# Moving a row copy from GpSimd to ScalarE, and a second buffer for a half of the hidden layer

## The chip, the cores and the metric

The kernel runs on one core of a Trainium2 chip. The metric is device time in microseconds (us): the median of several runs. The engines are called here as the profile calls them: PE (TensorE), DVE (VectorE), ACT (ScalarE), POOL (GpSimd) and SP, which issues loads. DMAs are issued from the queues of SP, ACT and POOL.

## The reference

Block-causal attention over 8 batches, 8 heads, 576 tokens and a head width of 64 gives 4608 rows of 512 values. A mixture of experts follows, with one expert out of 8 for each row:

```python
logits = x @ w_gate
expert_idx = np.argmax(logits, axis=1)
gate_w = probs[np.arange(N), expert_idx]
for e in range(E):
    mask = expert_idx == e
    h = np.maximum(x[mask] @ w1[e], 0.0)       # 512 -> 1024
    out[mask] = gate_w[mask, None] * (h @ w2[e])   # 1024 -> 512
```

All is fp32. The kernel keeps that accuracy by splitting each operand of the expert layers into a high part (a type that PE multiplies in one pass) and a low part (the rest), and adds three products: high by high, low by high, high by low.

## The kernel before

The first 366 us or so are attention, with the routing of each batch woven in; rows go to a table in DRAM (`xd`), sorted slots of 128 rows of one expert follow. The change lies in the second part, class `Experts`. It runs 38 slots in the profiled execution; slot `t` takes part in several **periods**, and `period(t)` (L1160) writes down the order of all engines by hand. Each engine's queue runs in that order, and counting semaphores tie the queues together.

In one period **PE** does 48 products of 512 columns and 4 transposes: `first_pe(t)` (L963, first layer of slot t, two halves of 12 into the banks `ph` and `o`), `second_pe(t-1, 0)` (L1086, 12 products of the second layer of the slot before), `hidden_pe(t, 1)` (L1059, turns the second half of the hidden values), and `second_pe(t-1, 1)`.

**The rows of a slot** come by `gather` (L874, an indirect DMA on POOL into one of four buffers `xg`), three periods ahead. From the sixth slot on (`TURNED` = 5) they are turned by DMA: POOL splits the 32-bit words into two 16-bit planes `xq` (`rows_planes`, L936), ACT issues the transposing DMA into `xt` (`rows_turned`, L945), POOL joins the planes again into `xf` (`rows_joined`, L951), ACT takes the high part (`rows_high`, L958) and POOL the low part (`rows_pool`, L925).

**The hidden values** (1024 per row) are two halves. The first half goes by DMA too: ACT's `planes` (L1023) reads `ph` and writes the planes into `h[0]`, `turned` (L1035) issues the transpose into `hf`, `joined` (L1046) writes the words back into `h[0]`, `joined_high` (L1053) takes the high part and the relu in place, and POOL subtracts the low part (`hidden_low`, L1080). The second half goes by `relu_act` (L1015) into `h[1]`, by `hidden_pe`, and by `hidden_act` (L1068), which reads the turned values from PSUM; POOL subtracts its low part first. Since `h[0]` is one buffer, `planes(t)` waits until POOL has finished the last low part of slot t-1 (`hp` at 2t).

The order of a period, from L1160 on:

- ACT: `out_act(t-2)` (L1114, scales the result by the gate), `planes(t)`, `turned(t)`, `relu_act(t, 1)`, `rows_high(t+1)`, `rows_turned(t+2)`, `hidden_act(t, 1)`, `joined(t)`, `joined_high(t)`.
- POOL: `out_pool(t-2)` (L1126, drain and the store by indirect DMA), `gather(t+3)`, `rows_joined(t+1)`, `gate(t+2)` and the planes of `rows_planes(t+2)`, `rows_pool(t+1)`, then the low parts of the second and of the first half.
- DVE splits each expert's weights (60 chunks, a cast for the high part at L1239, a subtraction for the low part at L1245), paced by PE's progress; SP loads them. POOL takes no part in that.

The last period is followed by `finish` (L1200): both halves of the last second layer, the last two stores.

Of the kernel before, what the change touches and what calls it, by code (L numbers as in the profile page):

```python
# [794 lines left out]
class Experts:  # L795
# [9 lines left out]
    def __init__(self, ctx, tc, ident, w1, w2, out, router, high, low, y, raw, ph):  # L805
        self.tc, self.nc, self.router = tc, tc.nc, router
        self.w1, self.w2, self.out, self.xd = w1, w2, out, router.xd
        self.ident, self.stab, self.nslot = ident, router.stab, router.nslot
        self.xg, meta = router.xg, router.meta
        self.e8, self.off, self.col, self.row, self.before = (*(meta[k] for k in ("e8", "off", "col", "row")), meta["si"])  # L810
        self.high, self.low = high, low
        self.hh, self.hl = low[:2], low[2:]
        sb = ctx.enter_context(tc.tile_pool(name="moe", bufs=1))
        ps = ctx.enter_context(tc.tile_pool(name="moeps", bufs=1, space=PSUM))

        def t(name, shape, dt=F32):
            return sb.tile(shape, dt, tag=name, name=name)

        self.w = t("w", [P, 2, 4, 4096], F32R)
        self.raw = raw  # L820
        self.idx = t("idx", [P, router.nslot + 2], I32)
        self.xf, self.xq, self.xt = t("xf", [P, 512]), t("xq", [P, 1024], U16), t("xt", [P, 1024], U16)
        self.gates = t("gates", [P, 8])
        self.h, self.hf = [t("h0", [P, 512]), t("h1", [P, 512])], t("hf", [P, 512])
        self.y = y

        def b(name):
            return ps.tile([P, 512], F32, tag=name, name=name)
# [28 lines left out]
    def run(self):  # L857
# [8 lines left out]
            )  # L866
        }
        sraw = [tc.alloc_semaphore(f"raw{i}") for i in range(nr)]
        sg = [tc.alloc_semaphore(f"g{i}") for i in range(4)]
        sy = tc.alloc_semaphore("y")  # L870
        pe, act, dve, pool, sp = nc.tensor, nc.scalar, nc.vector, nc.gpsimd, nc.sync
        wf = self.w.rearrange("p a b c -> p (a b c)")

        def gather(t):  # L874
            i = t % 4
            if t < EARLY or t >= NS:
                return
            if t == EARLY:
# [4 lines left out]
            c = pool.value_load(self.col[t : t + 1, 0:1], min_val=0, max_val=TC - 1)  # L883
            pool.tensor_copy(self.idx[:, t : t + 1], self.stab[:, bass.ds(c, 1)]).then_inc(sem["v1"], 1)  # L884
            pool.wait_ge(sem["v1"], t + 1 - EARLY)
            if t >= 4:
                pool.wait_ge(sem["gc"], t - 3)
                if t - 4 < TURNED:
                    pool.wait_ge(sem["xt"], t - 4)
                else:  # L890
                    pool.wait_ge(sem["xq"], t - 3 - TURNED)
            pool.indirect_dma_start(  # L892
                out=self.xg[i],
                out_offset=None,
# [3 lines left out]

        def gathered(t):

            return len([k for k in range(EARLY, t + 1) if k % 4 == t % 4])

        def rows_in(t):

            if t >= EARLY:
                pe.wait_ge(sg[t % 4], 16 * gathered(t))
            if t >= 2:
                pe.wait_ge(sem["xa"], 2 * t - 2)
            for k in range(4):
                m = pe.transpose(self.px[:, P * k : P * k + P], self.xg[t % 4][:, P * k : P * k + P], self.ident)  # L910
# [19 lines left out]

        def gate(t):
            if t >= EARLY:
                pool.wait_ge(sg[t % 4], 16 * gathered(t))
            pool.tensor_copy(self.gates[:, t % 8 : t % 8 + 1], self.xg[t % 4][:, GATE : GATE + 1]).then_inc(sem["gc"], 1)

        def rows_planes(t):  # L936
            gate(t)
            if t > TURNED:
                pool.wait_ge(sem["ti"], 16 * (t - TURNED))
            pool.tensor_copy(  # L940
                self.xq.rearrange("p (o c) -> p o c", o=2),
                self.xg[t % 4][:, 0:DM].bitcast(U16).rearrange("p (c o) -> p o c", o=2),
            ).then_inc(sem["xq"], 1)

        def rows_turned(t):  # L945
# [3 lines left out]
            act.dma_start_transpose(self.xt.rearrange("p (k c) -> p k c", c=P), self.xq).then_inc(sem["ti"], 16)  # L949

        def rows_joined(t):  # L951
            pool.wait_ge(sem["ti"], 16 * (t - TURNED + 1))
            pool.wait_ge(sem["xa"], 2 * t - 2)
            pool.tensor_copy(  # L954
                self.xf.bitcast(U16).rearrange("p (c o) -> p o c", o=2), self.xt.rearrange("p (o c) -> p o c", o=2)
            ).then_inc(sem["xj"], 1)

        def rows_high(t):  # L958
# [64 lines left out]
        def planes(t):  # L1023

            act.wait_ge(sem["mm1"], 2 * t + 2)
            if t == 2:
                act.wait_ge(sem["ht"], 3)
            else:
                act.wait_ge(sem["hp"], 2 * t)
            act.copy(  # L1030
                self.h[0].bitcast(U16).rearrange("p (o c) -> p o c", o=2),
                self.ph[0].bitcast(U16).rearrange("p (c o) -> p o c", o=2),
            ).then_inc(sem["ra"], 1)

        def turned(t):  # L1035
# [6 lines left out]
            act.dma_start_transpose(  # L1042
                self.hf.bitcast(U16).rearrange("p (k c) -> p k c", c=P), self.h[0].bitcast(U16)
            ).then_inc(sem["tr"], 16)

        def joined(t):  # L1046
            act.wait_ge(sem["tr"], 16 * (t - 1))
            act.copy(  # L1048
                self.h[0].bitcast(U16).rearrange("p (c o) -> p c o", o=2),
                self.hf.bitcast(U16).rearrange("p (o c) -> p c o", o=2),  # L1050
            ).then_inc(sem["jo"], 1)

        def joined_high(t):  # L1053
            act.wait_ge(sem["jo"], t - 1)
            act.wait_ge(sem["mm2"], t)
            act.activation(self.hh[t % 2][:, 0], self.h[0], AF.Relu).then_inc(sem["ha"], 1)  # L1056
            act.activation(self.h[0], self.h[0], AF.Relu).then_inc(sem["ha"], 1)

        def hidden_pe(t, f):  # L1059
            if t:  # L1060
# [19 lines left out]
        def hidden_low(t, f, engine):  # L1080
            n = f if t < 2 else 1 - f
            engine.wait_ge(sem["ha"], 4 * t + 2 * n + 2)
            hh, hl = self.hh[t % 2][:, f], self.hl[t % 2][:, f]
            engine.tensor_sub(hl, self.hf if t < 2 else self.h[f], hh).then_inc(sem["hp"], 1)  # L1084

        def second_pe(t, part):  # L1086
            e8, off = self.regs[t]
# [72 lines left out]
        def period(t):  # L1160
# [39 lines left out]
        def finish(t):  # L1200
# [10 lines left out]
            for i in range(4):  # L1211
                n = len([k for k in range(EARLY, min(last + 3, NS)) if k % 4 == i])
                if n:
                    pool.wait_ge(sg[i], 16 * n)

# [2 lines left out]
        with tc.tile_critical():  # L1218
# [34 lines left out]
            sp.dma_start(self.router.by_partition(last, GATE, GATE + 1), g[:, 0:4, None]).then_inc(sem["ga"], 16)  # L1253
            sp.dma_start(self.xd[t0 : t0 + 64, GATE : GATE + 1], g[0:64, 4:5]).then_inc(sem["ga"], 16)
            begin()
            for i in range(5):
                if i == 1:
                    rows_pool(1)
                self.router.scatter(last, i, posi).then_inc(sem["sc"], 16)
            rows_pool(2)  # L1260
            for t in range(EARLY):
                gate(t)
            gather(EARLY)
            for k in range(4):
                m = dve.tensor_copy(tuple(self.parts(0, k))[1], self.low[k].rearrange("p a b -> p (a b)"))
# [188 lines left out]
```

## Time and profile before

| what | value |
|---|---|
| median of 3 runs | 878.25 us (875.03 to 879.1) |
| the profiled execution's own time | 875.0 us |
| its span | 873.2 us |
| mean granted clock of PE | 0.981 of full speed |
| PE busy | 816.7 us, 94% |
| ACT busy | 541.9 us, 62% |
| POOL busy | 445.9 us, 51% |
| DVE busy | 437.2 us, 50% |

The span runs from the first to the last instruction, and 1.8 us lie around it. A timeline row has the start in us from the span's start, the length in us, the engine, the line, the operation, the tiles (out <- in) and how often it stands merged in the row; in brackets stands how long the engine was idle before it and what released it. `ACTq` is ACT's queue issuing a DMA. Ends of PE's matmuls are modelled, so PE is better read from start to start. A tile name loses its number: `h` is either buffer of the hidden half.

### The profile page before, as it was taken

To read this page: it belongs to the slowest core of one execution; us is meant where nothing else is said; L and a number is where in the kernel's file an instruction comes from. 1 tells how busy PE (TensorE), PEld (TensorE's weight loads), DVE (VectorE), ACT (ScalarE), POOL (GpSimd) and SP (SyncE) were. 2 spreads that over 40 slices of the span, in tenths; PEclk is the share of its full clock that TensorE was granted. 3 is DMA by queue.
4 is the path that set the end of the run, shared out by engine and by line. 5 is a ranking of instruction groups with operands and counts; after the bars stand their busy time and mean duration, and the time that the engine had idled before them with its cause. 6 is when DMAs were issued, how large, how long until landed. Compare 5 with 4: busy or idle time off the path is not lost.

```text
span 873.2 us, 16347 instructions
## 1 busy us (share of the span) xinstructions
PE 816.7 (94%) x4990; PEld 620.9 (71%) x4990; DVE 437.2 (50%) x1208; ACT 541.9 (62%) x1220; POOL 445.9 (51%) x503
## 2 busy tenths in 40 slices
PE   6999999999999999898999999897898989999995
PEld 5777777777777777686877777665676667777773
DVE  5778787878787877587064000367338523000000
ACT  6898899898988898344445544434353444554452
POOL 3000223333233222447776777676767777677763
PEclk8999999999999999999999999999999989999998
DMA  6254848372636281448558443569658663344342
GB/s 208 94 133 136 167 118 186 108 160 95 161 107 149 95 231 40 107 146 252 131 153 185 97 91 90 158 163 192 170 133 269 177 152 83 68 92 97 85 75 63
DMA packets 120747, 118.24 MB, mean 135 GB/s; under 512 B 82577, under 2 KB 85905, under 8 KB 120658
## 3 DMA queue, kind: packets, MB, share of 16 engines
q1 hardware_dynamic: 38082, 78.26, 31.9%
q10 hardware_dynamic: 74976, 18.62, 14.1%
q0 software_dynamic: 7600, 20.24, 7.2%
q8 instruction: 49, 0.80, 0.4%
q14 instruction: 40, 0.33, 0.1%
HBM read 77.02 MB, written 21.98 MB: 113 GB/s over the span
## 4 chain that ended last, share of the span: by engine, by line
PE 39%; POOL 22%; issue 15%; POOLq 7%; ACT 6%; ACTq 5%; DMA 2%; DVE 1%; DVEq 0%
PE o L305 11%; POOL low L1084 5%; POOLq L1127 5%; ACTq L949 5%; POOL xf L954 5%; PE ya L203 5%; POOL xg L892 4%; POOL xq L940 4%; PE xa L203 3%; PE py L1104 3%; PE o L340 2%; ACT h L1078 2%; DMA kd<-kT 2%; PE o L983 2%; PE ph L983 1%
## 5 line engine op out<-in xcount | busy, mean ns | idle before, releaser
L1104 PE MATMUL py<-w,low 128*128 (+1 forms) x912 | 231.3, 404 | 7.5 <-ACT low L1056 4.7
L1104 PEld LDWEIGHTS py<-w,low 128*128 128x128 f32 x912 | 171.5, 192 | 46.2 <-issue 8.3
L1239 DVE CAST w<-raw 128x1024 fp32r<-128x1024 f32 x60 | 58.3, 1021 | 196.5 <-PE o L983 136.0
L1084 POOL TENSOR_TENSOR low<-h,low 128x512 fp32r<-128x512 f32 x72 | 102.5, 1424 | 82.3 <-ACT h L1078 47.8
L248 POOL TENSOR_SCALAR p<-p,rs 128x64 f32<-128x64 f32 x32 | 14.2, 443 | 250.1 <-DVE rs L244 167.5
L983 PE MATMUL ph<-w,high 128*128 x408 | 107.7, 410 | 12.8 <-POOL high L929 6.5
L983 PEld LDWEIGHTS ph<-w,high 128*128 128x128 f32 x408 | 76.1, 193 | 40.0 <-POOL high L929 14.6
L983 PE MATMUL o<-w,high 128*128 x408 | 101.5, 398 | 0.0
L1245 DVE TENSOR_TENSOR w<-raw,w 128x1024 fp32r<-128x1024 f32 x60 | 91.3, 1579 | 2.2 <-PE o L983 2.2
L983 PEld LDWEIGHTS o<-w,high 128*128 128x128 f32 x408 | 77.8, 191 | 18.6
L961 ACT CAST high<-xf 128x512 fp32r<-128x512 f32 x34 | 21.1, 620 | 77.7 <-POOL xf L954 77.7
L1075 ACT CAST low<-pt 128x512 fp32r<-128x512 f32 x40 | 23.5, 588 | 72.8 <-issue 43.6
L1129 POOL DMA_INDIRECT out<-y,idx x35 | 43.0, 1229 | 44.0 <-issue 39.0
L1030 ACT COPY h<-ph 128x1024 uint16<-128x1024 uint16 x36 | 36.4, 1012 | 37.6 <-POOL low L1084 37.6
L1021 ACT ACTIVATE h<-o 128x512 f32<-128x512 f32 x37 | 22.1, 598 | 55.2 <-issue 45.2
L235 ACT ACTIVATE pb<-ya,neg 128x320 f32<-128x320 f32 (+2 forms) x93 | 48.5, 532 | 2.3 <-PE pt30x L274 1.6
L733 POOL DMA_INDIRECT tab<-toks,posi x40 | 41.6, 1041 | 15.1 <-issue 14.0
L235 ACT ACTIVATE pb<-yb,neg 128x320 f32<-128x320 f32 (+2 forms) x93 | 49.3, 544 | 0.0
L892 POOL DMA_INDIRECT xg<-xd,idx x38 | 43.5, 1145 | 10.5 <-POOL idx L884 10.5
L1048 ACT COPY h<-hf 128x1024 uint16<-128x1024 uint16 x36 | 42.6, 1183 | 7.8 <-DMA hf<-h 7.8
L929 POOL TENSOR_TENSOR high<-xf,high 128x512 fp32r<-128x512 f32 x35 | 45.7, 1305 | 2.7 <-ACT xf L923 2.7
L954 POOL COPY xf<-xt 128x1024 uint16<-128x1024 uint16 x34 | 47.0, 1383 | 0.0
(968 smaller groups left out, 2081.4 us busy)
## 6 DMA issues: line engine op xcount, KB each, us to landing
raw<-w SPq DMA_DIRECT2D x60, 512.0 KB, 5.4
qd<-qT SPq DMA_DIRECT2D x32, 352.0 KB, 2.8
v<-vt SPq DMA_DIRECT2D x32, 352.0 KB, 4.6
kd<-kT SPq DMA_DIRECT2D x32, 288.0 KB, 3.4
xd<-xt SPq DMA_DIRECT2D x7, 1026.0 KB, 11.0
xd<-xg SPq DMA_DIRECT2D x9, 256.5 KB, 7.2
xg<-w SPq DMA_DIRECT2D x8, 256.0 KB, 4.7
xd<-x SPq DMA_DIRECT2D x8, 128.0 KB
```

What stands on the lines that cost most here:

```text
L203: ins = mm(out, q[x][r, 128 * (i - 1) : 128 * i], q[y][r, o : o + w], start=n == 0, stop=n == 2, skip_group_check=True,)
L235: ins = self.nc.scalar.activation(dst, src, AF.Exp, bias=self.neg[m][:, c : c + 1], scale=1.0, accum_out=self.sums[m][:, c : c + 1])
L305: self.nc.tensor.matmul(out[r], self.raws[m][2][:, slot], self.ph[m, bank][:, c0:c1], start=t in (0, 5), stop=t in (4, 5), skip_group_chec ...
L892: pool.indirect_dma_start(out=self.xg[i], out_offset=None, in_=self.xd[:, :], in_offset=bass.IndirectOffsetOnAxis(ap=self.idx[:, t : t + 1 ...
L929: pool.tensor_sub(self.x(t, 1), self.xf, self.x(t, 0)).then_inc(sem["xp"], 1)
L949: act.dma_start_transpose(self.xt.rearrange("p (k c) -> p k c", c=P), self.xq).then_inc(sem["ti"], 16)
L954: pool.tensor_copy(self.xf.bitcast(U16).rearrange("p (c o) -> p o c", o=2), self.xt.rearrange("p (o c) -> p o c", o=2)).then_inc(sem["xj"], 1)
L983: m = pe.matmul(self.ph[f], x[:, P * k : P * k + P], weights(k, f, part), start=start and k == 0, stop=stop and k == 3,)
L1084: engine.tensor_sub(hl, self.hf if t < 2 else self.h[f], hh).then_inc(sem["hp"], 1)
L1104: m = pe.matmul(self.py[t % 2], h[:, c // 4, P * (c % 4) : P * (c % 4) + P], wf[:, bass.ds(off + (base + 512 * c), 512)], start=n == 0, st ...
L1239: dve.tensor_copy(hi, raw[m % nr]).then_inc(sem["wh"], 1)
L1245: dve.tensor_sub(lo, raw[m % nr], hi).then_inc(sem["wd"], 1)
```

## The change

`rows_joined` moves from POOL's queue to ACT's, ahead of `rows_high`, with its access pattern in the word order that `joined` uses. The first half of the hidden values alternates between `h[0]` and the memory of the fourth row buffer `xg[3]`; `planes(t)` waits for the low part of slot t-2 in place of t-1. The gathered rows take three buffers in turn instead of four. The three early gate copies stand ahead of the table's scatters, as the buffer of slot 0 is now the first to be gathered into.

```diff
+        self.hz = [self.h[0], self.xg[3][:, 0:512]]
...
         def gather(t):
-            i = t % 4
+            i = t % 3
...
-            if t >= 4:
-                pool.wait_ge(sem["gc"], t - 3)
-                if t - 4 < TURNED:
-                    pool.wait_ge(sem["xt"], t - 4)
-                else:
-                    pool.wait_ge(sem["xq"], t - 3 - TURNED)
+            pool.wait_ge(sem["gc"], t - 2)
+            if t - 3 < TURNED:
+                if t > 3:
+                    pool.wait_ge(sem["xt"], t - 3)
+            else:
+                pool.wait_ge(sem["xq"], t - 2 - TURNED)
...
         def rows_joined(t):
-            pool.wait_ge(sem["ti"], 16 * (t - TURNED + 1))
-            pool.wait_ge(sem["xa"], 2 * t - 2)
-            pool.tensor_copy(
-                self.xf.bitcast(U16).rearrange("p (c o) -> p o c", o=2), self.xt.rearrange("p (o c) -> p o c", o=2)
+            act.wait_ge(sem["ti"], 16 * (t - TURNED + 1))
+            act.wait_ge(sem["xp"], t - 1)
+            act.copy(
+                self.xf.bitcast(U16).rearrange("p (c o) -> p c o", o=2), self.xt.rearrange("p (o c) -> p c o", o=2)
             ).then_inc(sem["xj"], 1)
...
         def planes(t):
             act.wait_ge(sem["mm1"], 2 * t + 2)
-            if t == 2:
+            if t < 4:
                 act.wait_ge(sem["ht"], 3)
             else:
-                act.wait_ge(sem["hp"], 2 * t)
+                act.wait_ge(sem["hp"], 2 * t - 2)
             act.copy(
-                self.h[0].bitcast(U16).rearrange("p (o c) -> p o c", o=2),
+                self.hz[t % 2].bitcast(U16).rearrange("p (o c) -> p o c", o=2),
...
             elif more:
+                rows_joined(t + 1)
                 rows_high(t + 1)
...
-            if more and t + 1 >= TURNED:
-                rows_joined(t + 1)
...
             begin()
+            for t in range(EARLY):
+                gate(t)
             for i in range(5):
                 if i == 1:
                     rows_pool(1)
                 self.router.scatter(last, i, posi).then_inc(sem["sc"], 16)
             rows_pool(2)
-            for t in range(EARLY):
-                gate(t)
             gather(EARLY)
```

`turned`, `joined`, `joined_high` and `hidden_low` take `hz[t % 2]` in place of `h[0]` in the same way, and every other `% 4` of the row buffers becomes `% 3`.

## Rows read from the trace of the kernel before

**Rows 1.** Parts 1 and 2 of the page: busy us; busy tenths by slice

```profile
PE 816.7 (94%) x4990; PEld 620.9 (71%) x4990; DVE 437.2 (50%) x1208; ACT 541.9 (62%) x1220; POOL 445.9 (51%) x503
...
POOL 3000223333233222447776777676767777677763
```

**Rows 2.** Part 4 of the page: the chain that ended last, shares by engine

```profile
PE 39%; POOL 22%; issue 15%; POOLq 7%; ACT 6%; ACTq 5%; DMA 2%; DVE 1%; DVEq 0%
```

**Rows 3.** Timeline of PE: start, length, instruction, [idle before]; ph begins a period

```profile
411.59 2.95 PE L983 MATMUL ph<-w,high 128*128 x12
...
434.78 2.95 PE L983 MATMUL ph<-w,high 128*128 x12
...
446.37 2.95 PE L983 MATMUL ph<-w,high 128*128 x12
...
545.71 2.97 PE L983 MATMUL ph<-w,high 128*128 x12
...
730.15 3.36 PE L983 MATMUL ph<-w,high 128*128 x12
...
841.73 2.99 PE L983 MATMUL ph<-w,high 128*128 x12
...
858.64 8.53 PE L1104 MATMUL py<-w,low 128*128 x24 [4.65 <-ACT low L1056]
```

**Rows 4.** Timeline of POOL, one period without weight work

```profile
511.49 1.29 POOL L1084 TENSOR_TENSOR low<-h,low 128x512 fp32r<-128x512 f32 x1 [1.27 <-ACT h L1078]
...
513.74 1.29 POOL L1084 TENSOR_TENSOR low<-h,low 128x512 fp32r<-128x512 f32 x1 [0.95 <-ACT h L1057]
...
518.61 1.38 POOL L954 COPY xf<-xt 128x1024 uint16<-128x1024 uint16 x1
...
519.99 1.06 POOL L940 COPY xq<-xg 128x1024 uint16<-128x1024 uint16 x1
...
523.58 1.29 POOL L1084 TENSOR_TENSOR low<-h,low 128x512 fp32r<-128x512 f32 x1 [1.28 <-ACT h L1078]
```

**Rows 5.** Timeline of ACT, the same period

```profile
511.30 1.18 ACT L1048 COPY h<-hf 128x1024 uint16<-128x1024 uint16 x1
...
513.57 0.67 ACT L1122 ACTIVATE y<-py,gates 128x512 f32<-128x512 f32 x1
...
515.12 1.01 ACT L1030 COPY h<-ph 128x1024 uint16<-128x1024 uint16 x1 [0.89 <-POOL low L1084]
...
517.57 0.60 ACT L1021 ACTIVATE h<-o 128x512 f32<-128x512 f32 x1 [1.44 <-issue]
...
520.07 0.62 ACT L961 CAST high<-xf 128x512 fp32r<-128x512 f32 x1 [1.90 <-POOL xf L954]
...
521.08 1.25 ACTq L949 DMA_TRANSPOSE xt<-xq  x1
...
522.43 0.59 ACT L1075 CAST low<-pt 128x512 fp32r<-128x512 f32 x1 [1.74 <-PE py L1104]
```

**Rows 6.** Timeline of POOL, first and last low part of thirteen loops, one copy

```profile
547.77 1.30 POOL L1084 TENSOR_TENSOR low<-h,low 128x512 fp32r<-128x512 f32 x1 [1.28 <-ACT h L1078]
...
558.70 2.05 POOL L940 COPY xq<-xg 128x1024 uint16<-128x1024 uint16 x1
...
732.59 1.30 POOL L1084 TENSOR_TENSOR low<-h,low 128x512 fp32r<-128x512 f32 x1 [1.26 <-ACT h L1078]
```

**Rows 7.** Timeline of DVE, low parts of a weight chunk group

```profile
554.13 5.71 DVE L1245 TENSOR_TENSOR w<-raw,w 128x1024 fp32r<-128x1024 f32 x4
```

**Rows 8.** One stretch: PE, PEld, DVE, ACT, POOL busy; PEclk; DMA share

```profile
580.00:620.00 40.00, 32.66 (x135) 23.93 (x134) 23.91 (x19) 14.45 (x21) 27.54 (x25) 0.96 0.94 222
```

**Rows 9.** Tile hf (turned first half), 420 to 873: issue to landing

```profile
DMA to landing us min/median/max: 3.1/4.2/13.3
```

**Rows 10.** Tile xt (turned rows), 420 to 873: issue to landing

```profile
DMA to landing us min/median/max: 3.0/3.3/8.9
```

**Rows 11.** Timeline of POOL, the three early gate copies

```profile
377.95 0.43 POOL L934 COPY gates<-xg 128x1 f32<-128x1 f32 x3
```

More of the change, by code (lines that the diff above doesn't have):

```diff
@@ L868, in run @@
         sraw = [tc.alloc_semaphore(f"raw{i}") for i in range(nr)]
-        sg = [tc.alloc_semaphore(f"g{i}") for i in range(4)]
+        sg = [tc.alloc_semaphore(f"g{i}") for i in range(3)]
         sy = tc.alloc_semaphore("y")
@@ L899, in gathered @@
         def gathered(t):
-            return len([k for k in range(EARLY, t + 1) if k % 4 == t % 4])
+            return len([k for k in range(EARLY, t + 1) if k % 3 == t % 3])
         def rows_in(t):
             if t >= EARLY:
-                pe.wait_ge(sg[t % 4], 16 * gathered(t))
+                pe.wait_ge(sg[t % 3], 16 * gathered(t))
             if t >= 2:
@@ L909, in rows_in @@
             for k in range(4):
-                m = pe.transpose(self.px[:, P * k : P * k + P], self.xg[t % 4][:, P * k : P * k + P], self.ident)
+                m = pe.transpose(self.px[:, P * k : P * k + P], self.xg[t % 3][:, P * k : P * k + P], self.ident)
                 if t == 1 and k < 2:
@@ L932, in gate @@
             if t >= EARLY:
-                pool.wait_ge(sg[t % 4], 16 * gathered(t))
-            pool.tensor_copy(self.gates[:, t % 8 : t % 8 + 1], self.xg[t % 4][:, GATE : GATE + 1]).then_inc(sem["gc"], 1)
+                pool.wait_ge(sg[t % 3], 16 * gathered(t))
+            pool.tensor_copy(self.gates[:, t % 8 : t % 8 + 1], self.xg[t % 3][:, GATE : GATE + 1]).then_inc(sem["gc"], 1)
         def rows_planes(t):
@@ L941, in rows_planes @@
                 self.xq.rearrange("p (o c) -> p o c", o=2),
-                self.xg[t % 4][:, 0:DM].bitcast(U16).rearrange("p (c o) -> p o c", o=2),
+                self.xg[t % 3][:, 0:DM].bitcast(U16).rearrange("p (c o) -> p o c", o=2),
             ).then_inc(sem["xq"], 1)
@@ L1042, in turned @@
             act.dma_start_transpose(
-                self.hf.bitcast(U16).rearrange("p (k c) -> p k c", c=P), self.h[0].bitcast(U16)
+                self.hf.bitcast(U16).rearrange("p (k c) -> p k c", c=P), self.hz[t % 2].bitcast(U16)
             ).then_inc(sem["tr"], 16)
@@ L1048, in joined @@
             act.copy(
-                self.h[0].bitcast(U16).rearrange("p (c o) -> p c o", o=2),
+                self.hz[t % 2].bitcast(U16).rearrange("p (c o) -> p c o", o=2),
                 self.hf.bitcast(U16).rearrange("p (o c) -> p c o", o=2),
@@ L1055, in joined_high @@
             act.wait_ge(sem["mm2"], t)
-            act.activation(self.hh[t % 2][:, 0], self.h[0], AF.Relu).then_inc(sem["ha"], 1)
-            act.activation(self.h[0], self.h[0], AF.Relu).then_inc(sem["ha"], 1)
+            h = self.hz[t % 2]
+            act.activation(self.hh[t % 2][:, 0], h, AF.Relu).then_inc(sem["ha"], 1)
+            act.activation(h, h, AF.Relu).then_inc(sem["ha"], 1)
         def hidden_pe(t, f):
@@ L1083, in hidden_low @@
             hh, hl = self.hh[t % 2][:, f], self.hl[t % 2][:, f]
-            engine.tensor_sub(hl, self.hf if t < 2 else self.h[f], hh).then_inc(sem["hp"], 1)
+            engine.tensor_sub(hl, self.hf if t < 2 else (self.hz[t % 2], self.h[1])[f], hh).then_inc(sem["hp"], 1)
         def second_pe(t, part):
@@ L1210, in finish @@
             pool.wait_ge(sem["ti"], 16 * (min(last + 2, NS) - TURNED))
-            for i in range(4):
-                n = len([k for k in range(EARLY, min(last + 3, NS)) if k % 4 == i])
+            for i in range(3):
+                n = len([k for k in range(EARLY, min(last + 3, NS)) if k % 3 == i])
                 if n:
```

## The prediction

> **What bounds the kernel now.** I read the page first. PE is busy for 94% of the span and POOL for 51%, but POOL's busy tenths rise to 6 or 7 in the second half, where the expert layers run [rows 1]; the change lies there alone. The chain that ended last is not PE's alone: PE holds 39% of it, POOL 22%, and "issue" and the queues much of the rest [rows 2]. So the second half is a loop in which PE is one station. To see where it is tight I went to the timelines.
>
> PE first. Where nothing holds it, a period takes 446.37 - 434.78 = 11.59 us [rows 3]; that is PE's floor (48 products, 4 transposes, no idle time in the row). From 411.59 to 841.73 there are 33 periods, 430.14 us, while 33 floors are 382.5 [rows 3]. So **47.6 us** are lost to something other than PE, and PE waits once more, 4.65 us, ahead of the last second layer [rows 3].
>
> Then POOL in a quiet period, without weight work. Its first low part starts at 511.49 and again at 523.58: a loop of **12.09 us**, 0.5 above PE's floor [rows 4]. Followed around: the second low part ends at 515.03; drain, store, index and gather take it to 518.61 (3.58); the join takes 1.38 to 519.99; the planes end at 521.05; ACT's queue issues the transpose (521.08, 1.25), and only then comes `hidden_act`, which stands behind it in ACT's order, at 522.43; POOL's next low part starts at 523.58 [rows 4, 5]. POOL and ACT hold each other in turn; every piece lies on the chain, the join too.
>
> Last, the periods with weight work. From 547.77 to 732.59 POOL makes thirteen such loops in 184.82 us, 14.22 each [rows 6]. The planes copy that takes 1.06 in the quiet period takes 2.05 there, beside DVE's subtractions of weights [rows 4, 6, 7]. The stretch over 13 quiet loops is 184.82 - 13 x 12.09 = 27.7 us.
>
> **The change, part by part.**
>
> *The join leaves POOL.* It cuts 1.38 from the POOL chain, since the steps before and behind it follow without a wait [rows 4]. The quiet loop becomes 12.09 - 1.38 = **10.71**, under PE's floor by 0.88.
>
> *The join enters ACT.* The word-order copy that ACT makes already has the same size and pattern and takes 1.18 [rows 5]. It stands behind `relu_act` and ahead of `rows_high`, where ACT now idles 1.90 for POOL's join [rows 5]. In the present phase `relu_act` ends at 518.17; join and high part would end at 518.17 + 1.18 + 0.62 = 519.97, and POOL's planes, without the join, at 521.05 - 1.38 = 519.67. ACT is then 0.3 behind; that is gone because `planes` also starts earlier (next). ACT's whole round: 522.43 to 514.24 + 12.09 is 3.90; planes to relu, 515.12 to 518.17, 3.05; join 1.18; high part 0.62; issue 1.35 [rows 5]: 10.10, under 11.59. PE's work covers the join there; if that cover were gone it would cost up to 1.18 a period.
>
> *Two buffers for the first half.* `planes` no longer waits for the last low part. It can follow `out_act`, which ends at 514.24, and starts 0.88 earlier than 515.12 [rows 5]; so does `relu_act`, on which PE's transposes wait. What is late next is the first layer itself, on PE, which is the floor. The turned half has less time to land: from the end of `planes` (516.13) to its read (511.30 + 12.09) 7.26 now [rows 5], about 6.5 with PE as the bound, against a median landing of 4.2 and a longest of 13.3 [rows 9].
>
> *Three row buffers.* The gather's new condition is a copy two periods back on its own queue, so it adds no wait; queued behind it are planes and low parts, as before. POOL's queue reaches the planes 1.38 sooner; the rows asked for in the period before have then some 12 us in which to land. Cost 0.
>
> *Gate copies ahead of the scatters.* Three copies, 0.43 together [rows 11], delay scatters and the low part of slot 1's rows, and leave their old place. Between 0 and 0.43; I take 0, for the same 0.43 comes free before the first gather.
>
> **The sum.** In the thirteen weight loops POOL needs 184.82 - 13 x 1.38 = 166.9; PE's floor there is 150.7. POOL falls behind by 16.2, but it now starts ahead: with PE as the bound, `relu_act` runs right behind the first layer, at some 5.7 us of a period, and PE asks for it only after the next twelve products, at 8.4 (quarters of 2.8). From this order I estimate that POOL may lag 3.4 to 4.4 us before PE stops; I take 3.9. PE then needs 163.0 for the 13 periods from 545.71 to 730.15, which took 184.44 [rows 3]: **21.4 less**. The other 20 periods took 430.14 - 184.44 = 245.7; at the floor 231.8: **13.9 less**. At the end PE starts the last second layer 16.91 after its period began [rows 3]. With ACT right behind PE, relu, join, high part, issue, two copies, word join and high part run 5.7 + 0.6 + 1.18 + 0.62 + 1.35 + 1.0 + 1.2 + 0.6 = 12.2; I take 12.9, some issues being longer: **4.0 less**. Together 39.3. The profiled execution took 875.0, so 835.7; the median is 3.25 above it, so **839**.
>
> For the stretch I kept 27.7 us, because the other POOL instructions meet the same DVE work. The Trainium skill has a rule on it (SBUF — State Buffer, "Who interferes with whom"): GpSimd and a two-input VectorE instruction take their shared port pair in turns, and the second waits the first one out. By that rule each POOL instruction is a chance to be held; with one of about nine gone, up to a ninth of the stretch would go too, and the sum would be 836.
>
> The bounds: if POOL's lag never reached PE, 12.3 more would go (827). If POOL had no such lead, and the latest transpose cost what it exceeds 6.5 by, 3.9 and 6.8 come back (850) [rows 9].
>
> **The rivals.**
>
> *ACT becomes the bound.* ACT's instructions run in order: `hidden_act` at 522.43 waits until the issue before it is through [rows 5]. With the join in that line, a round of 10.10 plus 2 us of waits for PE's halves would be 12.1. For it: the round has many hand-overs. Against it: the waits fall where PE is ahead. Then the 20 other periods keep 245.7, the thirteen gain only 17.9 and the end 4.0: 853.1, **857** as a median. The Trainium skill says the same of the queue (TensorE: Matmul & The Clock Gate, on engine queue depths: ScalarE is strictly first in, first out); the rows agree in that the 0.59 copy starts only behind the 1.25 issue.
>
> *The weight periods keep their length,* because DVE and the loads hold them, not the join. For it: DMA share 0.94 and a mean clock of 0.96 between 580 and 620 [rows 8]. Against it: PE's waits there end with ACT or POOL. Gain 13.9 + 4.0: **860**.
>
> *Nothing changes,* because another wait fills the join's place, such as the gathered rows' landing before the planes. For it: that landing is asked for sooner. Against it: the planes follow at once. **878**.
>
> *Slower: the turned half comes late.* PE that runs faster draws the next expert's loads closer together while the transposes share the DMA engines. The place is `joined` in the weight periods, in ACT's order ahead of the result and of the next planes. If every one of the 13 landed as late as the latest, 13.3 [rows 9], 13 x (13.3 - 6.5) = 88 would come on top of -39: **927**. It decides from a mean landing of 9.5 in those periods (39 / 13 + 6.5). Against it: the median is 4.2, and the turned rows' longest is 8.9 [rows 9, 10].
>
> **How the numbers follow.** The forecast has 0.74, ACT as bound 0.08, unchanged weight periods 0.08, nothing 0.05, slower 0.05. The range 829 to 857 holds the forecast with nearly all of its bounds and the first rival. A measurement of this kernel tells 0.5% from no change, about 4.4 us. Faster by more than that is all of the first three, 0.90; same 0.05; slower 0.05.
>
> **What would show it.** Right: no xf copy on POOL, and one on ACT of about 1.2 us without waiting for POOL; quiet periods of 11.6 on PE without idle time before the transposes; POOL waiting in quiet periods; weight periods near 12.5; PE's last wait near 0.6. Wrong: quiet periods still near 12.1 with ACT busy or issuing throughout; `joined` waiting for its DMA in many periods; PE waits that end with weights.

## The result, and the profile after

The changed kernel took **839.98 us**, the median of four executions (834.12 to 843.06), beside 876.64 for the kernel before (873.84 to 879.1, four executions): a ratio of 0.9575, with a 95% interval from 0.9512 to 0.9638. The forecast was 839 with a range from 829 to 857. Ratios here and below leave out executions more than 1.5% above the fastest of their kernel; medians keep them. Line numbers move by a few: `rows_joined` is now ACT's L955, `rows_pool` L930, `hidden_low` L1086, `joined` L1049, `out_pool` L1131.

The profiled execution is the longest of the four, 843.06, with a span of 841.3; 31.9 less than the span before. The page, its parts 1, 2 and 4, answers to [rows 1, 2]:

```profile
PE 804.2 (96%) x4990; PEld 622.9 (74%) x4990; DVE 429.5 (51%) x1208; ACT 577.0 (69%) x1254; POOL 404.4 (48%) x469
...
POOL 3000133333333512263657666675777776666663
...
PE 19%; POOL 6%; issue 5%; POOLq 2%; ACTq 1%; ACT 1%; DMA 1%
```

ACT gains 34 instructions and 35 us, POOL loses 34 and 41.5. The chain that ended last had 39% of PE and 22% of POOL; now it is followed through far less of the span, and POOL's part falls to 6%. Shares of a chain say where the last waits lie, not how long a stage is, so the stages are read from PE's timeline, as in [rows 3]:

```profile
401.07 3.78 PE L984 MATMUL ph<-w 128*128 x8 [5.36 <-POOL w L930]
...
414.70 2.96 PE L984 MATMUL ph<-w,high 128*128 x12
...
499.73 2.95 PE L984 MATMUL ph<-w,high 128*128 x12
...
511.34 2.96 PE L984 MATMUL ph<-w,high 128*128 x12
...
522.97 2.95 PE L984 MATMUL ph<-w,high 128*128 x12
...
546.14 2.95 PE L984 MATMUL ph<-w,high 128*128 x12
...
620.22 1.08 PE L984 MATMUL ph<-w,high 128*128 x4
623.64 2.78 PE L984 MATMUL ph<-w,high 128*128 x8 [2.34 <-POOL high L930]
626.21 3.91 PE L984 MATMUL o<-w,high 128*128 x12
629.96 2.94 PE L1106 MATMUL py<-w,low 128*128 x12
...
635.97 2.95 PE L984 MATMUL ph<-w,high 128*128 x12
...
710.38 2.95 PE L984 MATMUL ph<-w,high 128*128 x12
...
814.79 2.95 PE L984 MATMUL ph<-w,high 128*128 x12
...
827.62 5.85 PE L1106 MATMUL py<-w,low 128*128 x24 [1.05 <-ACT xg L1059]
```

Quiet periods last 11.61 and 11.63 (499.73, 511.34, 522.97): PE's floor. Differences of such starts give the stages. The table has them for all profiled executions that the text compares by stages; the rows below "changed" are runs of the experiments below, `after_again` and `after_c` being the changed kernel itself.

| profiled execution | first period begins | 13 weight periods | other 20 | last period to last second layer | from there to the end | span |
|---|---|---|---|---|---|---|
| before | 411.59 | 184.44 | 245.70 | 16.91 | 14.56 | 873.2 |
| predicted | 411.59 | 163.0 | 231.8 | 12.9 | 14.56 | |
| changed | 414.70 | 164.24 | 235.85 | 12.83 | 13.68 | 841.3 |
| after_again | 414.20 | 161.84 | 235.17 | 12.83 | 13.56 | 837.6 |
| after_c | 414.08 | 166.69 | 232.43 | 12.55 | 12.65 | 838.4 |
| join_only | 411.48 | 164.04 | 233.96 | 12.86 | 13.96 | 836.3 |
| join_only_b | 416.96 | 160.15 | 232.86 | 12.57 | 12.96 | 835.5 |
| buffer_only | 416.10 | 182.52 | 250.17 | 16.45 | 13.36 | 878.6 |
| ring_only | 412.54 | 185.57 | 248.37 | 16.89 | 13.43 | 876.8 |
| gates_back | 411.87 | 164.88 | 233.17 | 12.98 | 13.20 | 836.1 |
| gates_back_b | 413.38 | 159.66 | 236.74 | 12.56 | 13.06 | 835.4 |
| dve_later | 411.30 | 166.40 | 232.49 | 12.54 | 13.07 | 835.8 |
| join_twice | 415.61 | 162.83 | 233.56 | 13.16 | 13.14 | 838.3 |
| low_twice | 418.21 | 171.65 | 242.32 | 12.61 | 13.71 | 858.5 |

Between before and changed the columns give +3.1, -20.2, -9.9, -4.1 and -0.9: the 31.9. Four things are to be seen.

**The loop.** ACT in a quiet period, to be held against [rows 5]; the last row belongs to the end, below:

```profile
514.34 1.01 ACT L1031 COPY h<-ph 128x1024 uint16<-128x1024 uint16 x1 [0.96 <-PE ph L984]
...
517.14 0.60 ACT L1022 ACTIVATE h<-o 128x512 f32<-128x512 f32 x1 [1.79 <-PE o L984]
517.63 1.17 ACT L955 COPY xf<-xt 128x1024 uint16<-128x1024 uint16 x1
518.88 0.62 ACT L962 CAST high<-xf 128x512 fp32r<-128x512 f32 x1
...
520.37 0.59 ACT L1077 CAST low<-pt 128x512 fp32r<-128x512 f32 x1 [0.88 <-PE pt L1067]
...
834.98 0.69 ACT L1124 ACTIVATE y<-py,gates 128x512 f32<-128x512 f32 x1 [5.79 <-DMA out<-y,idx]
```

The joined rows follow `relu_act` without a wait. Where ACT waited for POOL before (0.89 and 1.90), it waits for PE: 0.96, 1.79, 0.88. POOL's timeline has the same period in its fourth to sixth rows, to be held against [rows 4]; the first three rows are the start, the last two stand beside weight work:

```profile
381.52 0.90 POOL L885 COPY idx<-stab 128x1 int32 x1 [3.26 <-issue]
382.69 1.70 POOL L893 DMA_INDIRECT xg<-xd,idx  x1 [0.27 <-POOL idx L885]
...
393.61 2.00 POOL L1131 DMA_INDIRECT out<-y,first  x1 [9.22 <-issue]
...
510.62 1.30 POOL L1086 TENSOR_TENSOR low<-h,low 128x512 fp32r<-128x512 f32 x1 [1.28 <-ACT h L1080]
...
519.58 1.30 POOL L930 TENSOR_TENSOR high<-xf,high 128x512 fp32r<-128x512 f32 x1 [0.64 <-ACT high L962]
...
521.53 1.29 POOL L1086 TENSOR_TENSOR low<-h,low 128x512 fp32r<-128x512 f32 x1 [0.65 <-ACT h L1080]
...
619.34 2.04 POOL L941 COPY xq<-xg 128x1024 uint16<-128x1024 uint16 x1
621.35 2.23 POOL L930 TENSOR_TENSOR high<-xf,high 128x512 fp32r<-128x512 f32 x1
```

The loop of POOL and ACT can be read here by itself. From 510.62 to the next first low part at 521.53 it takes 10.91, and the three loops before took 10.83, 10.93 and 10.83 (POOL's timeline, from 478.03 on): POOL was catching up what it had lost earlier, while PE ran at its floor. The loop after it takes 11.59 (to 533.12), PE's pace. The wait of 0.64 for the high part is new; the other, 1.28, was there before.

**The weight periods.** Two of the thirteen hold 8.2 of the 13.6 us that they stand over their floors (164.24 - 13 x 11.59). In one, PE stopped at 620.22 + 1.08 for 2.34 us, until the low part of the rows was there: POOL's copy of the planes and its subtraction, 1.04 and 1.30 long in quiet periods, took 2.04 and 2.23. DVE subtracted weights at that time:

```profile
617.00 5.45 DVE L1246 TENSOR_TENSOR w<-raw,w 128x1024 fp32r<-128x1024 f32 x4
```

Then PE's clock was lower. The view of single stretches (columns as in [rows 8]) shows it:

```profile
624.00:628.00 4.00, 4.00 (x13) 3.13 (x12) 0.00 (x0) 3.52 (x5) 2.49 (x2) 0.61 1.20 189
...
632.00:636.00 4.00, 4.00 (x21) 3.25 (x21) 0.00 (x0) 3.12 (x5) 2.54 (x3) 1.00 0.70 163
```

A granted clock of 0.61 means most of that stretch at 1.2 GHz, not 2.4; eight us on it is back at 1.00. From start to start, the 8 and 12 products behind the wait took 2.57 and 3.75; at the 2.80 that twelve take in a quiet period they would take 1.87 and 2.80. So the wait costs 2.34, and the clock 1.65 on top. The second of the two (683.12 to 698.79, 15.67) is the same, with a wait of 2.35. The clock doesn't always follow: in `join_twice`, below, a wait of the same length in the same place left it at 1.00 over the next 4 us, and the 8 products took 1.96 from start to start:

```profile
619.71 2.12 PE L988 MATMUL ph<-w,high 128*128 x8 [2.36 <-POOL high L930]
```

The longest of the thirteen in `after_c`, 16.79, began otherwise. `joined` waited 6.89 for its turned half, and PE 3.35, up to 574.33, when the high parts of that half and of a weight chunk had come within 0.1 us of each other (timelines of PE, ACT and DVE).

**The end.** The last second layer waited 4.65 before and ran at 0.65 of the clock: 8.53 for 24 products [rows 3]. It now waits 1.05, and the same products take 5.85. That is 2.7 less, of which 1.5 are given back: the last result waits for a store of the one buffer `y` (ACT at 834.98), which is 1.5 after PE is through (827.62 + 5.85).

**The start.** The first period begins 3.1 later. Of these, 2.2 lie ahead of the products on which PE waits (401.07 against 398.85 before) and 0.9 behind it, where the clock was 0.50 over 4 us against 0.69. PE waits 5.36 for the low part `w` of slot 2's rows (first row of the fence on PE). POOL's timeline, above, shows what is ahead of it in the queue: the first store goes out at 393.61, though ACT's result was ready at 390.30; the drain before it ran for 10.28 us, to 392.8. In the kernel before, the store went out at 390.74, 0.86 behind ACT's result.

### The profile page after: what moved, and what is told of

It reads as the page before. It is cut to its first block, busy times and chain, and to the rows that moved or that the text cites. A ratio compares the mean times of both kernels' runs of the same rounds, so it can differ in the third digit from the quotient of the medians.

```text
span 841.3 us, 16347 instructions
## 1 busy us (share of the span) xinstructions
PE 804.2 (96%) x4990; PEld 622.9 (74%) x4990; DVE 429.5 (51%) x1208; ACT 577.0 (69%) x1254; POOL 404.4 (48%) x469
## 5 line engine op out<-in xcount | busy, mean ns | idle before, releaser
L1106 PE MATMUL py<-w,low 128*128 (+1 forms) x912 | 227.5, 399 | 2.4 <-issue 1.4
L1106 PEld LDWEIGHTS py<-w,low 128*128 128x128 f32 x912 | 168.8, 189 | 40.6 <-issue 3.7
L984 PE MATMUL ph<-w,high 128*128 x408 | 104.4, 403 | 8.3 <-POOL high L930 8.3
L1086 POOL TENSOR_TENSOR low<-h,low 128x512 fp32r<-128x512 f32 x54 | 74.5, 1380 | 57.0 <-ACT h L1080 32.4
L1246 DVE TENSOR_TENSOR w<-raw,w 128x1024 fp32r<-128x1024 f32 x60 | 84.4, 1464 | 3.2 <-PE o L984 3.2
L1131 POOL DMA_INDIRECT out<-y,idx x35 | 41.5, 1185 | 43.1 <-issue 36.2
L930 POOL TENSOR_TENSOR high<-xf,high 128x512 fp32r<-128x512 f32 x35 | 49.3, 1408 | 19.0 <-ACT high L962 16.1
L893 POOL DMA_INDIRECT xg<-xd,idx x38 | 45.0, 1184 | 10.6 <-POOL idx L885 9.9
L220 DVE TENSOR_REDUCE neg<-ya 128x1 f32<-128x320 f32 (+2 forms) x93 | 44.8, 482 | 0.0
L220 DVE TENSOR_REDUCE neg<-yb 128x1 f32<-128x320 f32 (+2 forms) x93 | 41.9, 478 | 3.3 <-ACT pb L235 1.3
L340 PE MATMUL o<-fold,oT 128*128 128x144 f32 x256 | 42.2, 288 | 1.0 <-ACT oT L312 0.6
L941 POOL COPY xq<-xg 128x1024 uint16<-128x1024 uint16 x35 | 41.3, 1179 | 0.9 <-DMA xt<-xq 0.9
```

The source lines that it names most:

```text
L220: ins = self.nc.vector.tensor_reduce(self.neg[m][:, c : c + 1], src, AX.XY if i == 4 else AX.X, ALU.max, negate=True)
L340: mm(t[:, i], self.oT[m, 0][:, o : o + P], w, start=True, stop=True)
L893: pool.indirect_dma_start(out=self.xg[i], out_offset=None, in_=self.xd[:, :], in_offset=bass.IndirectOffsetOnAxis(ap=self.idx[:, t : t + 1 ...
L930: pool.tensor_sub(self.x(t, 1), self.xf, self.x(t, 0)).then_inc(sem["xp"], 1)
L941: pool.tensor_copy(self.xq.rearrange("p (o c) -> p o c", o=2), self.xg[t % 3][:, 0:DM].bitcast(U16).rearrange("p (c o) -> p o c", o=2),).t ...
L984: m = pe.matmul(self.ph[f], x[:, P * k : P * k + P], weights(k, f, part), start=start and k == 0, stop=stop and k == 3,)
```

## The experiments

The theory after the first result: the join on POOL's loop was the whole limit of the quiet periods, and the rest of the change is neutral. Rivals: the second buffer gives POOL the lead that the forecast counted on; ACT is now close to being the bound; the early gate copies delay the start. Runs of one chip are compared with the kernel before on that chip: `join_only`, `buffer_only`, `ring_only` and `order2` ran on one, `join_twice`, `low_twice`, `gates_back` and `after_again` on a second, the next three on a third, and `dve_later` by itself.

**One part at a time.** `join_only` is the kernel before with the join on ACT and nothing else:

```diff
-            pool.wait_ge(sem["xa"], 2 * t - 2)
-            pool.tensor_copy(
+            act.wait_ge(sem["xp"], t - 1)
+            act.copy(
...
+                rows_joined(t + 1)
                 rows_high(t + 1)
```

> The kernel before with one part of the change: the join moves to ACT ahead of rows_high; one buffer for the first half, four row buffers. Theory (the join was a piece of the loop of POOL and ACT): the quiet loop becomes about 10.9 us, under PE's floor of 11.59, so most of the gain stands, 840 to 850 us. Rival (the second buffer carries the gain, since planes still waits for the last low part): quiet periods near 12 us on PE, time 860 or more.

Measured: 836.37 (833.13 to 844.81), ratio 0.9541 [0.9434, 0.9648]: the whole gain, and a time under the 840 to 850 that was expected. Its quiet periods on PE:

```profile
505.94 2.96 PE L983 MATMUL ph<-w,high 128*128 x12
...
517.57 2.95 PE L983 MATMUL ph<-w,high 128*128 x12
```

11.63, the floor, with one buffer for the first half. `buffer_only` is the changed kernel with `rows_joined` back on POOL's queue, as in the kernel before:

> The changed kernel with the join put back on POOL: two buffers for the first half, three row buffers, early gate copies. Theory: POOL's loop keeps its 12.09 us, since no piece of it is taken away; PE's waits ahead of the transposes vanish but turn up elsewhere; 872 to 879 us, no change that can be told. Rival (the buffer carries the gain): the 14.7 us that PE waited for relu_act go, 862 us or less.

Measured: 874.05 (868.55 to 880.34, ten executions) beside 879.4, ratio 0.996 [0.9926, 0.9994]. The quiet periods last 12.09, as before (PE's timeline), and ACT waits for POOL's join 34 times, 114.3 us in all (the view of waits, ACT: total us, times, longest):

```profile
507.84 3.46 PE L984 MATMUL ph<-w,high 128*128 x12
...
519.93 3.45 PE L984 MATMUL ph<-w,high 128*128 x12
```

```profile
ACT high L962 <- POOL xf L955: 114.3, 34, 5.1
```

So `planes` starts earlier and next to nothing is won, 0.4%, with an interval that ends just short of no change: ACT comes to POOL's join sooner and waits for it. `ring_only` is the kernel before with three row buffers and the early gate copies (`hz` holds `h[0]` twice):

```diff
+        self.hz = [self.h[0], self.h[0]]
...
-            i = t % 4
+            i = t % 3
```

> The kernel before with three row buffers in turn and the early gate copies alone. Theory: no wait is added, 876 us within 0.5%. Rival (the ring of three or the gate copies cost): over 881 us, with POOL waiting in the gather or in front of the gate copy, or a later start of the expert layers.

Measured: 878.09, ratio 0.9995 [0.9957, 1.0033]. The ring costs nothing that can be measured. Its first store, though, was late as well: 3.1 behind the result.

**How close ACT and POOL are.** `join_twice` makes ACT's join twice in a row in each period, writing the same values:

```diff
+            act.copy(
+                self.xf.bitcast(U16).rearrange("p (c o) -> p c o", o=2), self.xt.rearrange("p (o c) -> p c o", o=2)
+            ).then_inc(sem["tw"], 1)
+            act.wait_ge(sem["tw"], t - TURNED + 1)
```

> The changed kernel with ACT's join made twice (the same copy again, behind a wait for the first), which adds some 1.3 us to every ACT round and leaves the output as it is. Theory (ACT's round of 10.1 us has 1.5 to spare under PE's 11.59, and in the quiet periods the join is not on the path): quiet periods stay at 11.6 on PE; only in the weight periods ACT is then later than POOL's planes, by about 1 us a loop; 843 to 853 us. Rival (ACT is the bound now, or nearly): quiet periods of 12.2 or more, 860 us or more.

Measured: 840.2 (838.39 to 847.25), under the expected 843 to 853, ratio 0.9601 [0.9522, 0.9679]; 841.5 for the changed kernel beside it. The second copy costs nothing in the quiet periods, as ACT's timeline shows:

```profile
516.25 1.16 ACT L955 COPY xf<-xt 128x1024 uint16<-128x1024 uint16 x1
517.44 1.18 ACT L959 COPY xf<-xt 128x1024 uint16<-128x1024 uint16 x1
518.70 0.62 ACT L966 CAST high<-xf 128x512 fp32r<-128x512 f32 x1
```

A cost in the weight periods didn't show either (162.83 for the thirteen, 161.84 to 166.69 without): ACT has at least another 1.18 us to spare, and is not the bound. `low_twice` does the like to POOL's neighbour: DVE makes each of its 60 subtractions of weights twice:

```diff
+                dve.tensor_sub(lo, raw[m % nr], hi).then_inc(sem["tw"], 1)
+                dve.wait_ge(sem["tw"], twice)
                 dve.tensor_sub(lo, raw[m % nr], hi).then_inc(sem["wd"], 1)
```

> The changed kernel with DVE's low part of every weight chunk made twice (the same subtraction, behind a wait for the first): 60 more subtractions of about 1.4 us. Theory (what is left over PE's floor is POOL held by DVE's weight work): POOL's loops in the weight periods stretch by another 1 to 2 us, PE's waits for POOL and the periods over 13 us become more, quiet periods stay at 11.6; 850 to 870 us. Rival (the rest is late transposes and the clock, not DVE's work): within 1% of the changed kernel, 832 to 848 us.

Measured: 859.5 (856.87 to 862.7), ratio 0.98 [0.9729, 0.987]; 18 us over the changed kernel beside it. The view of PE's waits, of the changed kernel and of this one:

```profile
PE ph L984 <- POOL high L930: 8.3, 7, 2.4
```

```profile
PE ph L984 <- POOL high L930: 21.9, 11, 4.0
```

Quiet periods stay at 11.6. Of the 20.9 us between the two spans, 9.8 lie in the thirteen periods, 7.2 in the other twenty (one of 18.46 beside weight work, from 477.66) and 4.0 at the start. So POOL held up beside DVE, with PE waiting for the low part of the rows, is what costs most over the floor; late transposes come on top, as the period of `after_c` shows.

**The order of issue.** `order2` puts `rows_turned` last in ACT's period and the low part of the rows ahead of the planes in POOL's, so that PE gets its rows sooner:

```diff
-            if TURNED <= t + 2 < NS:
-                rows_turned(t + 2)
...
             joined_high(t)
+            if TURNED <= t + 2 < NS:
+                rows_turned(t + 2)
...
-            if TURNED <= t + 2 < NS:
-                rows_planes(t + 2)
             if more:
                 rows_pool(t + 1)
+            if TURNED <= t + 2 < NS:
+                rows_planes(t + 2)
```

> The changed kernel with another order: on ACT rows_turned goes behind joined_high, on POOL rows_pool goes ahead of rows_planes. Theory (what is left is POOL's loop beside weight work, with the issue of the transpose on it, and two falls of the clock behind PE's waits of 2.3 us for the low part of the rows): the quiet loop becomes about 9.2 us, the 8.3 us of PE's waits for the low part of the rows and most of the two slow periods (15.7 us each) go, 824 to 832 us. Rival (the turned rows then land too late, since they are issued some 3 us later): ACT waits in rows_joined in the weight periods, 838 us or more.

Measured: 848.11 (835.8 to 855.19, five executions), over the expected 824 to 832, ratio 0.9548 [0.9456, 0.9639] for the three shortest: unclear against the changed kernel. The profiled execution is the longest of the five, so its time isn't put on the order. ACT's waits in it:

```profile
ACT xf L955 <- DMA xt<-xq: 29.3, 8, 7.6
```

The rows, issued later, were waited for eight times, the longest landing being 12.6; in the changed kernel the same wait comes to 1.9 in two. That would be the rival's sign, but whether the shorter executions wait like this isn't shown. The order was not taken further.

**The start.** `gates_back` is the changed kernel with the three gate copies at their old place, behind the scatters; `after_again` is the changed kernel once more, beside it.

```diff
-            for t in range(EARLY):
-                gate(t)
             for i in range(5):
...
             rows_pool(2)
+            for t in range(EARLY):
+                gate(t)
```

> The changed kernel with the three early gate copies back behind the low part of slot 2's rows; ring of three and two buffers stay. Theory A (the gate copies ahead of the scatters make POOL's first store late): the first store starts within 1 us of ACT's scaled result again, the 3 us at the start of the expert layers go, 835 to 838 us. Theory B (the ring of three, with its gather into the first buffer, does it): the store still starts some 3 us behind the result, 840 us.

> The changed kernel itself, beside the three above on the same chip. All theories: 836 to 844 us; its profile shows which of the first one's losses come back: the late first store (over 2 us behind ACT's result) and one to three periods over 15 us in the weight work.

Measured: 837.08 (830.34 to 846.9), ratio 0.9502 [0.9413, 0.9591], and 841.5 (838.7 to 847.71), 0.9616 [0.9539, 0.9694]. The first store goes out 0.85 behind the result in the one and 3.5 behind in the other. So far the copies' place seemed to be the cause. The three candidates ran again side by side, `join_only_b` and `gates_back_b` being the same kernels as before:

> The kernel before with nothing but the join moved to ScalarE, side by side with the whole change on one chip. Theory (the join is the whole gain, the buffer and the ring add nothing, the early gate copies cost 3 us): 836 to 839, 2 to 4 us under the whole change; its interval overlaps that of the whole change. Rival (the second buffer gives POOL a lead that PE needs): 842 or more, above the whole change.

> The whole change, with the gate copies at their old place. Theory: as join alone, 836 to 839; the first period begins near 411.9. Rival (buffer worth something): 3 us or more under join alone. If the start's 3 us is given back later: equal to the whole change, 840.

> The changed kernel as it is, as the mark for the two others: 840 to 842 by both theories; the first period begins near 414.7, the first store some 3 us behind the result.

Measured: 837.91 [0.9538, 0.9615], 839.63 [0.9562, 0.9627] and 841.32 [0.9582, 0.9663] (medians of six, intervals of the ratio; the second is 0.6 over what was expected). The order is that of the theory, but the intervals overlap: 3.4 us between the first and the last are not shown. And the theory of the copies fell: in `join_only_b`, with the copies at their old place, the store is late too. In `gates_back_b` the store goes out in time, 0.86 behind the result, but the first period begins at 413.38, not near 411.9. POOL's timeline of `join_only_b`, and then that of `gates_back_b`; the changed kernel's rows stand in the section above:

```profile
383.53 1.16 POOL L884 COPY idx<-stab 128x1 int32 x1 [3.06 <-issue]
384.96 1.70 POOL L892 DMA_INDIRECT xg<-xd,idx  x1 [0.27 <-POOL idx L884]
395.01 0.99 POOL L1129 DMA_INDIRECT out<-y,first  x1 [8.34 <-issue]
```

```profile
381.83 0.27 POOL L885 COPY idx<-stab 128x1 int32 x1 [2.79 <-issue]
382.60 1.46 POOL L893 DMA_INDIRECT xg<-xd,idx  x1 [0.51 <-POOL idx L885]
391.44 1.50 POOL L1131 DMA_INDIRECT out<-y,first  x1 [7.37 <-ACT y L1124]
```

The small copy `idx`, ahead of the first gather, sorts them. DVE's first weight subtraction starts at 383.43, 381.97 and, in the changed kernel, 381.16; a subtraction of hidden values, 0.69 long, ends just ahead of it. In all fourteen profiles `idx` ends 0.04 or 0.05 behind the DVE subtraction during which it began (1.22 long for one of weights, as the single rows of `low_twice` have it). Where that is the subtraction of hidden values, `idx` takes 0.20 to 0.36 and the drain behind the gather 7.7 to 8.1 (before, `join_only`, `gates_back`, `gates_back_b`). Where it is the first one of weights, `idx` starts 0.1 to 0.4 behind the start of the weight work, takes 0.90 to 1.16, and the drain 9.4 to 10.6 (eight profiles, `join_only_b` among them). `low_twice` alone fits only half: `idx` 1.07, drain 8.2; there DVE's work is another. The last run tests it: gate copies ahead of the scatters as in the changed kernel, but DVE makes a 0.69 us subtraction of hidden values a second time, so that its weight work starts later:

```diff
+            dve.wait_ge(sem["ha"], 4)
+            dve.tensor_sub(self.hl[0][:, 1], self.hf, self.hh[0][:, 1]).then_inc(sem["tw"], 1)
+            dve.wait_ge(sem["tw"], 1)
             hidden_low(0, 1, dve)
```

> The changed kernel, gate copies still ahead of the scatters, with one 0.69 us subtraction of VectorE made a second time just ahead of its first weight subtractions, so that those begin some 0.7 us later and the small copy idx on GpSimd begins ahead of them instead of behind. Theory (the late first store is a matter of where idx falls against VectorE's subtractions, not of the gate copies): idx takes 0.2 to 0.4 us, the drain 7.7 to 8.2 instead of 9.4 to 10.6, the first store follows ScalarE's result by 0.8 to 0.9, the first period begins near 411.9, and the time is 837 to 840. Rival (the gate copies' place itself makes the drain late): drain 9.4 or more, first store 3 behind, first period near 414.7, time 840 to 842.

Measured, on POOL's timeline:

```profile
382.28 0.55 POOL L885 COPY idx<-stab 128x1 int32 x1 [3.24 <-issue]
383.11 1.70 POOL L893 DMA_INDIRECT xg<-xd,idx  x1 [0.27 <-POOL idx L885]
392.11 1.38 POOL L1131 DMA_INDIRECT out<-y,first  x1 [7.30 <-ACT y L1124]
```

DVE's timeline has the second of the doubled subtractions, and the weight work behind it:

```profile
382.10 0.69 DVE L1086 TENSOR_TENSOR low<-hf,low 128x512 fp32r<-128x512 f32 x1
382.71 2.35 DVE L1246 TENSOR_TENSOR w<-raw,w 128x1024 fp32r<-128x1024 f32 x2
```

`idx` begins 0.43 ahead of the weight work, but within that doubled subtraction, and ends 0.04 behind it; so it takes 0.55, and not the 0.2 to 0.4 expected. The drain takes 8.33, also a little more than expected, and the store follows 0.86 behind the result, with the copies where the change put them. So the store's delay goes by where `idx` meets DVE, and not by the copies' place itself.

That this delay costs the start its 3 us isn't shown. The first period begins at 411.30, 2.8 to 3.4 ahead of the three profiles of the changed kernel, but PE's products behind its wait begin only 0.2 to 1.2 ahead of theirs; the other 1.6 to 2.7 lie behind that, where PE's clock stayed at 1.00 over the next 4 us and was 0.50 to 0.57 in those three. In `gates_back_b`, with its store in time, it was 0.50. PE's timeline, of `dve_later` and of `gates_back_b`:

```profile
400.15 2.12 PE L984 MATMUL ph<-w 128*128 x8 [3.70 <-POOL w L930]
```

```profile
399.61 3.78 PE L984 MATMUL ph<-w 128*128 x8 [3.20 <-POOL w L930]
```

The time, 841.37 (834.37 to 841.6), is 1.4 over the expected range, but the kernel before took 880.34 on that chip: the ratio is 0.9543 [0.9499, 0.9587], the lower side of the changed kernel's.

No version beats the changed kernel by more than the intervals; `join_only` does the same with two edits.

## Why the prediction was right, and where it wasn't

**Right: the join's way off POOL.** The quiet loop was to fall under PE's floor, and did; ACT's copy was to take 1.18, and took 1.16 (median of 34). The loop of POOL and ACT was to take 10.71, and took 10.8 to 10.9 where PE didn't hold it. `join_only` has the whole gain, `buffer_only` at most 0.7%, and `join_twice` that ACT's round has the cover claimed for it. The rivals "ACT becomes the bound" and "nothing changes" fell with it. (The first one's sum is off by 0.6: 853.1 and 3.25 make 856.4, not 857.)

**Right in size, for a reason that isn't shown: the thirteen weight periods.** Predicted 163.0, profiled 164.24, 161.84 and 166.69. The step "it now starts ahead" leaned in part on the second buffer, by which `planes` and `relu_act` were to start 0.88 earlier. That part failed: `planes` now waits for PE (0.96 in a quiet period), and `join_only`, with one buffer, has 164.04 and 160.15. So the lead, if it is one, needs no second buffer. What the buffer does was seen in single periods only: a transpose of `hf` that was waited for 5.41 us made a period of 19.06 in `join_only`, where `planes` then waited another 2.33 for POOL; waits of 4.25 and 4.87 made periods of 13.38 and 13.85 in the changed kernel. Its times don't show it.

The stretch was kept at 27.7 us, and losses were to come from POOL's lag alone, 12.3 over the floors. Of the 13.6 measured in the profiled execution, PE's waits for the rows' low part are 7.0 and the clock behind the two long ones some 3.3 (an estimate: 1.65 twice); the period of 13.38, with a transpose that came late, adds 1.8. Neither the clock nor late transposes were priced. The sum came out because these made up for what POOL's lag cost less: in that the number was lucky.

The Trainium skill's rule (SBUF — State Buffer, "Who interferes with whom") would have given 836; the measured median, 840, doesn't separate it from 839. Its mechanism agrees with the rows: POOL's 1.04 and 1.30 become 2.04 and 2.23 beside DVE, and in `low_twice` PE waits 13.6 us longer for POOL's subtraction.

**Mis-sized: the other 20 periods.** "At the floor 231.8: 13.9 less". Measured 235.85, 235.17 and 232.43, so 9.9 to 13.3 less. In the profiled execution 3.8 of the 4.1 missing lie in two periods, 426.34 to 440.19 (the late `hf`, 4.87) and 451.82 to 464.95 (a wait of 1.27 for the rows' low part): 13.85 and 13.13. The floor was right, but not for all twenty.

**Missed: the start, "I take 0" for the gate copies.** It cost 3.1 in the profiled execution. The two ends of the bound, 0 and 0.43, counted the copies' own time, and neither the moment at which POOL's next work meets DVE's nor PE's clock behind the wait. That the copies' move did it isn't shown: with them at their old place the first period began anywhere from 411.48 to 416.96, and `join_only_b`, with 416.96, has one of the shortest spans.

**Right: the end,** 12.9 forecast and 12.83 measured; the last wait is 1.05, where 0.6 was named as the sign. Behind it lay a gain and a loss that were not counted, 2.7 from the clock and 1.5 to the store of `y`.

**The slower rival** wanted a mean landing of 9.5 for the turned half. `joined` waited for its DMA twice in the whole stretch, 9.1 us together (once, 6.9, in `after_c`; three times, 3.3, in `after_again`), so it fell. Of the signs of being wrong, a wait of PE that ends with weights came once in the three profiles, in the period of `after_c` above.

The sum was 39.3; the profiled span fell by 31.9, the median of all executions by 36.7. The time is right within 1 us because the sum was 2.6 too large and 839 was reckoned from a median of 878.25, 1.6 above the 876.64 that the kernel before came out at beside the changed one. So close a hit is luck; the fall itself is not.

## What to carry to other kernels

When two engines hold each other in a loop just over a third engine's floor (12.09 against 11.59), move the one step that both wait for; a buffer that lets one of them start earlier mostly moves the wait, as in `buffer_only`. When you price a stop of PE, look at the clock behind it too: a wait of 2.34 us cost 4.0 here, and one of 2.36 elsewhere hardly more than itself. And tenths of a microsecond in the moment at which one queue meets its neighbour's work can matter, so look at the moments, not only at durations; but follow such a delay up to the engine that bounds the kernel before you put a loss on it.

## What the hardware showed that was not expected

- **A few tenths decide 2 us.** GpSimd's 128-element copy `idx` ended 0.04 or 0.05 us behind the VectorE subtraction during which it began, in all fourteen profiles (with 1.22 us for one of weights). It took 0.20 to 0.36 when that was a subtraction of hidden values about to end and 0.90 to 1.16 when it was the first one of weights, and the drain behind the next indirect DMA took 7.7 to 8.1 against 9.4 to 10.6 (8.2 in `low_twice`, the exception). The Trainium skill says that a VectorE instruction with two SBUF inputs contends with a GpSimd instruction that reads SBUF, and that of two that contend the one issued first goes first while the other waits (SBUF — State Buffer, "Who interferes with whom"); the copy agrees with that. The Trainium skill also says that GpSimd can't write the descriptors of its own DMAs while VectorE runs in a two-port mode (SBUF — State Buffer, "SBUF: two separate sides"). No run here shows descriptors being written, so why the drain grows by more than the copy stays open.
- **The clock fell after short waits, but not always.** Stops of PE of 2.34 and 2.35 us were followed by granted clocks of 0.61 and 0.66 over 4 us, with 1.65 us lost in the one. Stops of 2.33 to 2.36 were followed by 1.00 in `gates_back` (683.13), `gates_back_b` (682.95) and `join_twice` (619.71), and by 0.63 to 0.58 in `after_again` (683.09), `dve_later` (682.05) and, later in the same profile, `join_twice` (683.70). Longer ones differ as well: 1.00 behind 3.70 in `dve_later`, 0.50 behind 3.20 in `gates_back_b`. So the length of the stop alone doesn't tell; what does stays open.
